# First values ahead of the bias rows on GpSimd's queue, queries first, two weight blocks in halves, and a new order of steps

**Chip and metric.** One core of one Trainium2 chip. The metric is the device time of one execution in microseconds (us). A "look" is one profiled run, of which the start and duration of every instruction are known. "Full rate" and "half rate" name two speeds of the matrix array that are read from durations here: the same fill matmul takes 0.39 us in one stretch and 0.61 us in another.

## The reference, cut to what matters

```python
# attention: B, H, S, D = 8, 8, 576, 64
scores = q @ k.T / 8 + bias_table[bucket(|i - j|)]       # T5 relative bias, per head
attn   = softmax(scores);  x = (attn @ v) as [4608, 512]
# feed-forward, d_ff = 1536
out = ((x @ w_a) * (x @ w_b)) @ w_out
```

The kernel works on bf16. It takes exp of the scores without the bias on ScalarE and multiplies by exp(bias) on VectorE. These factors ("band rows") are loaded from a small table that the kernel itself writes to memory at the start.

## The kernel before

All loads that change fp32 to bf16 are issued from GpSimd's queue, in the order of the tokens that begin with `<`. The other tokens are steps, issued in this order to each engine.

```python
wa_sb = [wpool.tile([128, NMC, WC], BF16, name=f"wa{i}") for i in range(NW)]   # 3 blocks of 512 columns
trb = ps_tr.tile([128, 1024], BF16, tag="tr", name="trb")   # one PSUM tile, used by halves for transposes
# ... cut: helpers
opening = """
    <k0 <q0 <k1 <q123h0 <k23 <tk <W0 <v0 <W1 <vtb <vta <tq <W2 <R0 <v1 <Wta <q123h1 <W3 <Wtb <R1
    <wa0 <k4 <wb0 <R2 <R3 <q4 <k5 <uq <q7 <q5 <wa1 <wb1 ...
    TK0 PC0:A TQ0 ... CK0:A CQ00:D w1 S001 ... E001 E000 ... M001 ... V0:D M101 ... AV00 N00 ...
    ... FA0a N01 HA0a ... FB0a ... FO00 FO01 FO02 HO0 CX70:D CX71:D
"""
```

The tokens that matter: `q0`, `k0`, `v0` are loads of batch 0 (number = head pair or half). `W0..W3` and `R0..R3` are band rows of a pair. `tq`, `tk`, `vta`, `vtb` are tails (the last 64 of 576 positions). `wa0`, `wb0` are weight blocks. `TQ`/`TK`/`TZ`/`X` transpose on TensorE into PSUM (fast memory that TensorE writes to), for the most part into `trb`. `CQ`/`CK`/`CZ`/`CX` copy the result out on ScalarE (`:A`) or VectorE (`:D`). `S` is scores, `E` exponentials (ScalarE), `M` band multiplications (VectorE), `V` a copy of values, `P` pads (writing zeros), `AV` attention times values, `N` its normalisation. `FA`/`FB` are feed-forward products with w_a and w_b, `FO` with w_out, and `wN` is N fill matmuls on zeros.

The softmax here doesn't subtract the row's maximum and nothing guards it: scores larger than these inputs give would overflow.

Of the kernel before, what the change touches and what calls it, by code (L numbers as in the profile page):

```python
# [13 lines left out]
def kernel(  # L14
# [11 lines left out]
    nc = tc.nc  # L26
    FP32 = mybir.dt.float32
    BF16 = mybir.dt.bfloat16
# [13 lines left out]
    NMC = DM // 128  # L42
# [4 lines left out]
    wpool = ctx.enter_context(tc.tile_pool(name="wpool", bufs=1))  # L47
# [17 lines left out]
    half = NB // 2  # L65
# [40 lines left out]

    NW = 3
    WC = DF // NW
    wa_sb = [wpool.tile([128, NMC, WC], BF16, name=f"wa{i}") for i in range(NW)]
    wb_sb = [wpool.tile([128, NMC, WC], BF16, name=f"wb{i}") for i in range(NW)]  # L110
    wo_sb = wpool.tile([128, NDF, DM], BF16, name="wo")
    tab_sb = wo_sb[:, :, :].rearrange("p a b -> p (a b)")[:, 0:TB]
    xn_sb = [wpool.tile([128, NT], BF16, name=f"xn{mc}") for mc in range(NMC)]
# [32 lines left out]
    def load_qh(h0, h1, h):  # L146
        nc.gpsimd.dma_start(
            out=qn[0][64 * h:64 * h + 64, 256 * h0:256 * h1].rearrange("p (h x) -> p h x", x=256),
            in_=q[0, h0:h1, 256 * h:256 * h + 256, :].rearrange("h (p t) d -> p h (t d)", t=NM))
# [4 lines left out]
    def load_v(b, h0, h1):  # L154
        load4(v, vn[b % 2], b, h0, h1)

    def load_compact(b, i):
        nc.gpsimd.dma_start(out=tlc[b][:, i, :].rearrange("r (h d) -> r h d", d=Dh),
                            in_=(q, k)[i][b, :, SM:S, :].transpose([1, 0, 2]))
# [23 lines left out]
    def load_w_out():  # L183
        nc.gpsimd.dma_start(out=wo_sb[:, :, :], in_=moe_w_out.rearrange("(t p) n -> p t n", p=128))
# [32 lines left out]
    def pad_x(i, eng):  # L217
# [5 lines left out]
                        in_=bass.AP(tensor=bias_table.tensor, offset=(NB - 1) * H,  # L223
                                    ap=[[0, NB], [1, H]]))
# [21 lines left out]
    c0 = S - 1 - NR // 2  # L246
# [4 lines left out]
    def load_w(hp, y0, y1):  # L251
        nc.gpsimd.dma_start(out=W_sb[hp][:, :, y0:y1],
                          in_=bass.AP(tensor=tab, offset=2 * hp * TB + y0,
                                      ap=[[NM, 128], [TB, 2], [1, y1 - y0]]))
# [4 lines left out]
    def load_wt(hh):  # L259
        nc.gpsimd.dma_start(out=Wt_sb[64 * hh:64 * hh + 64, :, 64:256],  # L260
                            in_=bass.AP(tensor=tab, offset=hh * TB + 512,
                                        ap=[[1, 64], [2 * TB, H // 2], [1, 192]]))

    def load_vt_part(b, hh):
        nc.gpsimd.dma_start(
            out=vt[b % 2][64 * hh:64 * hh + 64, hh, :, 0:Dh],
            in_=v[b, hh:H:2, SM:S, :].transpose([1, 0, 2]))

    def load_weights(src, dst, part):
        nc.gpsimd.dma_start(  # L270
            out=dst[part][:, :, :],
            in_=src[:, WC * part:WC * part + WC].rearrange("(m p) n -> p m n", p=128))

    def load(name):
        if name[0] in "qk" and name[1:2].isdigit():
            ps, _, half = name[1:].partition("h")
            p0, n = int(ps[0]), len(ps)
            if half:
                load_qh(2 * p0, 2 * p0 + 2 * n, int(half))
            else:  # L280
                b, h = divmod(2 * p0, H)
                (load_q if name[0] == "q" else load_k)(b, h, h + 2 * n)
        elif name[0] in "tu":
            load_compact(int(name[0] == "u"), int(name[1] == "k"))
        elif name in ("v0", "v1"):
            load_v(0, 4 * int(name[1]), 4 * int(name[1]) + 4)
        elif name[:3] == "vb1":
            load_v(1, *((0, 4) if name[3] == "a" else (4, 8)))
        elif name[:2] == "vt":
            load_vt_part(int(name[2] == "1"), "ab".index(name[-1]))  # L290
        elif name == "wo":
            load_w_out()
        elif name[:2] == "Wt":
            load_wt("ab".index(name[2]))
        elif name[0] in "WR":
            load_w(int(name[1]), *((320, NY) if name[0] == "W" else (0, 320)))
        else:
            load_weights(*((moe_w_a, wa_sb) if name[1] == "a" else (moe_w_b, wb_sb)), int(name[2]))

    st = [dict() for _ in range(NP)]  # L300

# [248 lines left out]
    def av(p, jqs):  # L550
        av_mm(p, jqs)
        av_norm(p, jqs)
# [71 lines left out]
    def ff_bank(name):  # L624
        ff["n"] += 1
        if ff["late"] and ff["n"] % 4 >= 2:
            return ps_sc.tile([128, 2, 512], FP32, tag="sc", name=name)[:, 0, :]
        return ps_ff.tile([128, 512], FP32, tag="ffn", name=name)

    def ff_in(w, kind, c, df, lo, n):  # L630
        ps = ff_bank(f"{kind}{c}_{df}_{lo}")
        for mc in range(NMC):
            nc.tensor.matmul(out=ps[:, 0:n], lhsT=w[df // 4][:, mc, 128 * (df % 4):128 * (df % 4) + 128],  # L633
                             rhs=xn_sb[mc][:, 512 * c + lo:512 * c + lo + n],
                             start=(mc == 0), stop=(mc == NMC - 1))
        ff[kind, df, lo] = ps
# [8 lines left out]
    def ff_a(c, df, lo=0, n=512):  # L645
        ff_in(wa_sb, "pa", c, df, lo, n)
        ff_ha(c, df, lo, n)

    def ff_b(c, df, lo=0, n=512):
        ff_in(wb_sb, "pb", c, df, lo, n)  # L650
        ff_g(c, df, lo, n)
# [66 lines left out]
    def v_next(s):  # L718
# [7 lines left out]
    ACT = nc.scalar  # L726

    opening = """
        <k0 <q0 <k1 <q123h0 <k23 <tk <W0 <v0 <W1 <vtb <vta <tq <W2 <R0 <v1 <Wta <q123h1 <W3 <Wtb <R1
        <wa0 <k4 <wb0 <R2 <R3 <q4 <k5 <uq <q7 <q5 <wa1 <wb1 <k6 <uk <vt1b <k7 <vb1a <vb1b <vt1a <wa2 <q6  # L730
        <wb2 <wo TK0 PC0:A TQ0 PF1:D PX1:D PV1:A PU0:D CK0:A CQ00:D w1 S001 PX0:D CQ01:A S000 E001 E000
        w1 TQ30 PC1:D TK1 CK1:D TQ10 CQ10:D S011 E011 CQ30:D TK3 S100 E100 TZ1 CK3:D S301 M001 TQ20
        PV0:D TK2 E301 S101 E101 CQ20:D CK2:D w1 S200 E200 CZ1:D M000 w1 KS w1 S201 EK w2 S010 E201 V0:D
        M101 TZ0 M100 M200 M201 AV00 N00 CZ0:A AV10 E010 X00 CX00:A S300 E300 N10 T0 V1:D X10 CX10:A
        M010 ET0 AV20 TQ11 TQ21 M011 N20 CQ11:A S110 S111 CQ21:A E110 X20 M301 TQ31 M300 AV30 T1 PW:D
        MT0 AV01 CX20:D M110 E111 N30 ET1 X30 M111 CQ31:A T2 ET2 S210 CX30:D E210 PF0:A LH FA0a N01 HA0a
        MT1 TK4 X01 T3 AV11 ET3 CX01:D S211 PU1:D FB0a FA1a E211 CK4:D HA1a N11 X11 G0a M210 S310 MT2
        CX11:A E310 FB1a G1a S311 FA2a HA2a TQ4 M211 CQ4:A FB2a AV21 E311 FA3a HA3a TQ5 MT3 M310 S43 S42
        CQ5:A G2a FB3a N21 M311 TK5 E43 E42 TZ0x G3a CZ0x:D AV31 LV CK5:D N31 FA4a HA4a X21 TQ7 CQ7:A
        S41 E41 S52 E52 CX21:D FB4a FA5a HA5a X31 G4a TK6 M43 FB5a CX31:D S40 E40 S53 G5a FA0b FB0b  # L740
        CK6:D M41 TZ1x HA0b G0b CZ1x:D S51 FA1b FB1b E53 M53 HA1b G1b E51 TK7 CK7:D M40 FA2b HA2b S50
        E50 FB2b FA3b G2b HA3b V2:D T4 FB3b FA4b V3:D ET4 G3b S70 E70 M42 MT4 M52 HA4b FB4b G4b TQ6 T5
        ET5 M50 CQ6:A AV40 N40 MT5 M51 FA5b S71 E71 HA5b S73 FB5b AV41 G5b M70 N41 S72 E73 FA6f E72 T6
        M73 M71 HA6f FB6f G6f AV50 N50 S62 ET6 MT6 E62 S61 FA7f HA7f M62 AV51 N51 TH S60 E61 M61 FB7f
        G7f E60 M60 S63 E63 M63 FA8f HA8f M72 T7 FB8f G8f AV60 N60 ET7 MT7 FA9f HA9f FB9f G9f AV70 FA10f
        FB10f N70 HA10f G10f AV71 FA11f N71 FB11f X71 HA11f G11f AV61 N61 X70 FO00 FO01 FO02 HO0 CX70:D
        CX71:D
    """

    h0 = (0, 1)  # L750
# [2 lines left out]
    def step(token):  # L753
# [5 lines left out]
        if token[0] == "<":  # L759
            load(token[1:])  # L760
            return
# [4 lines left out]
        if kind in ("FA", "HA", "FB", "G"):  # L766
            unit = (0, int(num[:-1]), 256 if num[-1] == "b" else 0, 512 if num[-1] == "f" else 256)
            if kind in ("FA", "FB"):
                ff_in(*((wa_sb, "pa") if kind == "FA" else (wb_sb, "pb")), *unit)
                nxt += 1  # L770
            else:
                (ff_ha if kind == "HA" else ff_g)(*unit)
            return
# [82 lines left out]
    for s in range(8, NP + 1):  # L856
        new = s < NP
        U = "unit"
        A = lambda *jq: (lambda: av(s - 1, jq) if s > 8 else None)
# [20 lines left out]
        b = s // 4 + 1  # L880
# [13 lines left out]
        for x in steps:  # L894
            if x is U:
                seen += 1
                n = (quota * seen + nu - 1) // nu - put
# [35 lines left out]
```

## Time and profile before

| | before |
|---|---|
| time, median of 4 runs | 413.96 us (413.32 to 414.21) |
| span of the profiled run | 412.2 us |
| TensorE busy | 404.5 us, one wait after 30 us (0.17 us, at 224.36) |
| first band multiplication | 11.69 us |
| first attention-value product / first feed-forward matmul | 17.32 / 26.55 us |
| first product with w_out (end of the opening list) | 70.65 us |

After the opening list both programs are the same. A win in the opening should therefore move the end by that much, unless it is given back inside the list. The profile lines behind the table stand in the prediction, but for that of the end of the list (TensorE), which stands behind it, and that of the multiplication (VectorE):

```profile
11.69 0.69 DVE L461 TENSOR_TENSOR ath<-ath,W 128x1024 bf16<-128x1024 bf16 x1
```

```profile
70.65 2.75 PE L670 MATMUL po<-wo,g 128*128 128x512 bf16 x12
...
224.36 1.02 PE L633 MATMUL pb<-xn,wb 128*128 128x512 bf16 x4 [0.17 <-DVE g L643]
```

### The profile page before, as it was taken

The numbers are of one execution on the slowest core, as the hardware profiler recorded it, in microseconds if no ns is written. First come the engines' busy times: TensorE is split into PE (matmuls) and PEld (weight loads), VectorE is DVE, ScalarE is ACT, GpSimd is POOL, SyncE is SP. The second block draws the span as 40 slices with busy tenths as digits, with TensorE's granted clock in tenths as the row PEclk, the third lists the DMA queues.
The fourth block names the chain that finished last, engine by engine and source line by source line (L and its number), as shares of the span: only waits on it lengthen the run. The fifth ranks groups of instructions, "written<-read, shape, count | busy, mean of one in ns | idle before, by whom it ended". The sixth has DMA issues, their size and how long they took to land.

```text
span 412.2 us, 8768 instructions
## 1 busy us (share of the span) xinstructions
PE 404.5 (98%) x3473; PEld 210.0 (51%) x3473; DVE 240.8 (58%) x568; ACT 251.3 (61%) x384; POOL 133.6 (32%) x191
## 2 busy tenths in 40 slices
PE   8999999999999999999999999999999999999996
PEld 3576656455555455455444555555545554444443
DVE  3898997366745665476656764667547652421320
ACT  4998992676748665677556765767486642322321
POOL 6967547788029300960079004300000000000000
PEclk9999999999999999999999999999999999999999
DMA  8999999999979914995299709960520012002004
GB/s 104 179 202 189 206 166 144 160 193 142 87 133 159 139 34 91 155 129 90 41 161 143 116 16 126 127 92 17 117 67 16 17 40 78 0 9 95 2 2 102
DMA packets 135786, 42.05 MB, mean 102 GB/s; under 512 B 113688, under 2 KB 130968, under 8 KB 135744
## 3 DMA queue, kind: packets, MB, share of 16 engines
q0 software_dynamic: 81712, 20.27, 56.3%
q1 hardware_dynamic: 48592, 11.87, 18.6%
q10 hardware_dynamic: 5440, 9.34, 7.2%
q8 instruction: 27, 0.44, 0.5%
q14 instruction: 15, 0.12, 0.1%
HBM read 39.18 MB, written 9.45 MB: 118 GB/s over the span
## 4 chain that ended last, share of the span: by engine, by line
PE 94%; DVE 2%; ACT 2%; DMA 1%; issue 1%; ACTq 0%; POOL 0%; POOLq 0%
PE pb L633 23%; PE pa L633 23%; PE po L670 22%; PE av L569 8%; PE qk L406 7%; PE av L559 2%; PE av L563 2%; PE qkh L446 1%; PE qkt L479 1%; DMA qn<-in_q_dram 1%; PE trb L321 1%; ACT ath L452 1%; PE trb L415 1%; PE trb L609 0%; DVE ath L461 0%
## 5 line engine op out<-in xcount | busy, mean ns | idle before, releaser
L430 ACT ACTIVATE at<-qk 128x1024 bf16<-128x1024 f32 x112 | 113.3, 1028 | 27.5 <-DMA out_dram<-ob 10.3
L643 DVE TENSOR_TENSOR g<-pb,ha 128x512 bf16<-128x512 f32 (+1 forms) x114 | 75.6, 664 | 75.0 <-PE pb L633 58.9
L633 PE MATMUL pb<-xn,wb 128*128 128x512 bf16 (+1 forms) x456 | 112.1, 368 | 0.2 <-DVE g L643 0.2
L633 PE MATMUL pa<-xn,wa 128*128 128x512 bf16 (+1 forms) x456 | 112.1, 368 | 0.0
L640 ACT ACTIVATE ha<-pa 128x512 f32<-128x512 f32 (+1 forms) x114 | 66.2, 581 | 67.7 <-PE pa L633 66.2
L670 PE MATMUL po<-wo,g 128*128 128x512 bf16 x420 | 98.2, 379 | 0.0
L435 DVE TENSOR_TENSOR at<-at,W 128x1024 bf16<-128x1024 bf16 x112 | 75.1, 686 | 22.2 <-ACT at L430 22.1
L633 PEld LDWEIGHTS <-wa 128*128 128x128 bf16 x456 | 41.2, 98 | 46.3 <-issue 6.6
L633 PEld LDWEIGHTS <-wb 128*128 128x128 bf16 x456 | 40.6, 97 | 43.6 <-issue 5.2
L670 PEld LDWEIGHTS <-g 128*128 128x128 bf16 x420 | 38.9, 98 | 44.9 <-issue 2.5
L675 ACT ACTIVATE ob<-po 128x512 f32<-128x512 f32 x34 | 20.4, 600 | 39.9 <-PE po L670 33.6
L569 PE MATMUL av<-vm,at 128*128 128x65 bf16 x896 | 41.2, 193 | 0.0
L569 PEld LDWEIGHTS <-at 128*128 128x128 bf16 x896 | 37.4, 97 | 6.3
L132 POOL DMA_DIRECT2D qn<-in_q_dram x48 | 36.4, 807 | 12.0 <-PE qk L406 6.9
L170 POOL DMA_DIRECT2D vt<-in_v_dram x12 | 7.4, 620 | 98.9 <-PE av L563 98.1
L580 DVE RECIPROCAL rc<-av 128x6 f32<-128x6 f32 (+1 forms) x64 | 11.9, 186 | 45.2 <-PE av L569 40.8
L141 POOL DMA_DIRECT2D kn<-in_k_dram x48 | 36.2, 794 | 1.4 <-issue 0.7
L559 PE MATMUL av<-vt,att 128*128 128x130 bf16 x152 | 33.6, 221 | 0.0
L406 PE MATMUL qk<-QB,KB 64*128 64x512 bf16 x192 | 29.1, 381 | 0.0
L582 DVE TENSOR_TENSOR XG<-av,rc 128x384 bf16<-128x384 f32 (+2 forms) x64 | 27.2, 425 | 2.2
L506 ACT ACTIVATE att<-qkt 128x640 bf16<-128x640 f32 x24 | 16.8, 701 | 13.0 <-PE qkt L480 13.0
L559 PEld LDWEIGHTS <-att 128*128 128x128 bf16 x152 | 15.0, 98 | 6.5
(104 smaller groups left out, 327.0 us busy)
## 6 DMA issues: line engine op xcount, KB each, us to landing
out_dram<-ob ACTq DMA_DIRECT2D x31, 256.0 KB, 3.1
vn<-in_v_dram POOLq DMA_DIRECT2D x16, 256.0 KB, 5.8
kn<-in_k_dram POOLq DMA_DIRECT2D x48, 64.0 KB, 5.0
qn<-in_q_dram POOLq DMA_DIRECT2D x48, 64.0 KB, 4.4
wa<-in_moe_w_a_dram POOLq DMA_DIRECT2D x3, 512.0 KB, 7.4
wb<-in_moe_w_b_dram POOLq DMA_DIRECT2D x3, 512.0 KB, 9.2
wo<-in_moe_w_out_dram POOLq DMA_DIRECT2D x1, 1536.0 KB, 15.6
xn<-XG SPq DMA_TRANSPOSE x52, 3.0
```

The source lines that it names most:

```text
L132: nc.gpsimd.dma_start(out=by_tile(qn[b % 2])[:, h0 // 4, t, :, :], in_=q[b, h0:h1, 128 * t:128 * t + 128, :].transpose([1, 0, 2]))
L141: nc.gpsimd.dma_start(out=by_tile(kn[b % 2])[:, h0 // 4, t, :, :], in_=k[b, h0:h1, t:SM:NM, :].transpose([1, 0, 2]))
L406: nc.tensor.matmul(out=ps[:, hh, :], lhsT=kT[r, t, :], rhs=qT[r, :, :], start=True, stop=True)
L430: nc.scalar.activation(out=at[:, :, :], in_=ps[:, :, :], func=ACTF.Exp, scale=scale)
L435: nc.vector.tensor_tensor(out=at[:, :, :], in0=at[:, :, :], in1=w[:, :, S - 1 + t:S - 1 + t - SM:-1], op=MULT)
L559: nc.tensor.matmul(out=pav[:, slot, :, :], lhsT=weights_tail(p, jq), rhs=vt[i][:, :, hp, :], start=True, stop=True)
L569: nc.tensor.matmul(out=pav[:, slot, hh, :], lhsT=weights(p, t, hh, jq), rhs=vm[i][:, 2 * hp + hh, t, :], start=False, stop=True, skip_grou ...
L582: nc.vector.tensor_tensor(out=xg[:, jqs[0]:jqs[0] + m, :, :], in0=pav[:, 0:m, :, 0:Dh], in1=rc[:, 0:m, :].unsqueeze(3).to_broadcast([128, ...
L633: nc.tensor.matmul(out=ps[:, 0:n], lhsT=w[df // 4][:, mc, 128 * (df % 4):128 * (df % 4) + 128], rhs=xn_sb[mc][:, 512 * c + lo:512 * c + lo ...
L640: nc.scalar.activation(out=ha[:, 0:n], in_=ff["pa", df, lo][:, 0:n], func=ACTF.Copy)
L643: nc.vector.tensor_tensor(out=g_sb[df][:, lo:lo + n], in0=ff["pb", df, lo][:, 0:n], in1=ff["ha", df, lo][:, 0:n], op=MULT)
L670: nc.tensor.matmul(out=po[:, :], lhsT=g_sb[df][:, 128 * tt:128 * tt + 128], rhs=wo_sb[:, df, :], start=(df == 0), stop=(df == NDF - 1))
```

## The change

The intent: with the values there early, the copy of values and all multiplications follow one another without a wait. The bias table's write (GpSimd waits 2.66 us for it) is covered by more loads. The first half of the first w_a block and of the first w_b block comes in time for an earlier feed-forward start.

```diff
-    wa_sb = [wpool.tile([128, NMC, WC], BF16, ...) for i in range(NW)]
+    wa_sb = [wpool.tile([128, 1 + (i == 0), NMC, WC // (1 + (i == 0))], BF16, ...) for i in range(NW)]
     (wb_sb alike; load_weights and ff_in index the halves)
     opening = """
-    <k0 <q0 <k1 <q123h0 <k23 <tk <W0 <v0 <W1 <vtb <vta <tq <W2 <R0 <v1 <Wta <q123h1 <W3 <Wtb <R1
-    <wa0 <k4 <wb0 <R2 <R3 <q4 <k5 <uq <q7 <q5 <wa1 <wb1 ...
+    <q0 <k0 <q123h0 <tk <k1 <k23 <tq <v0 <W0 <W1 <W2 <vta <W3 <q123h1 <vtb <R0 <v1 <Wta <Wtb <wa0a
+    <k4 <R1 <wb0a <R2 <k5 <q4 <wa0b <q5 <uq <wb0b <R3 <q7 <wa1 <vt1b <wb1 ...
-    TK0 PC0:A TQ0 ... CK0:A CQ00:D w1 S001 PX0:D CQ01:A S000 E001 E000 ...
+    PC0:D PF1:A PV0:D w1 TQ0 PU0:A PU1:D TK0 CQ00:A CQ01:A PX1:A CK0:D w1 S001 PV1:D E001 TQ10 ...
+    ... V0:D S200 E200 w2 S201 E201 M000 M001 w2 S300 ... (cut: the same steps in another order,
+    9 fill matmuls instead of 7, 13 copies and pads on the other engine)
+    ... TK5 S42 E311 G2a S43 M310 N21 CK5:D FB3a CZ0x:A FA4a ...
```

More of the change, by code (lines that the diff above doesn't have):

```diff
@@ L108 @@
     WC = DF // NW
-    wa_sb = [wpool.tile([128, NMC, WC], BF16, name=f"wa{i}") for i in range(NW)]
-    wb_sb = [wpool.tile([128, NMC, WC], BF16, name=f"wb{i}") for i in range(NW)]
+    wa_sb = [wpool.tile([128, 1 + (i == 0), NMC, WC // (1 + (i == 0))], BF16, name=f"wa{i}")
+             for i in range(NW)]
+    wb_sb = [wpool.tile([128, 1 + (i == 0), NMC, WC // (1 + (i == 0))], BF16, name=f"wb{i}")
+             for i in range(NW)]
     wo_sb = wpool.tile([128, NDF, DM], BF16, name="wo")
@@ L267, in load_vt_part, with load_weights @@
             in_=v[b, hh:H:2, SM:S, :].transpose([1, 0, 2]))
-    def load_weights(src, dst, part):
+    def load_weights(src, dst, part, half):
+        c0 = WC * part + WC // 2 * half
+        n = WC // (1 + (part == 0))
         nc.gpsimd.dma_start(
-            out=dst[part][:, :, :],
-            in_=src[:, WC * part:WC * part + WC].rearrange("(m p) n -> p m n", p=128))
+            out=dst[part][:, half, :, :],
+            in_=src[:, c0:c0 + n].rearrange("(m p) n -> p m n", p=128))
     def load(name):
@@ L297, in load @@
         else:
-            load_weights(*((moe_w_a, wa_sb) if name[1] == "a" else (moe_w_b, wb_sb)), int(name[2]))
+            load_weights(*((moe_w_a, wa_sb) if name[1] == "a" else (moe_w_b, wb_sb)), int(name[2]), int(name[-1] == "b"))
     st = [dict() for _ in range(NP)]
@@ L628, in ff_bank, with block @@
         return ps_ff.tile([128, 512], FP32, tag="ffn", name=name)
+    def block(w, df, mc):
+        half, d = divmod(df % 4, 2) if df < 4 else (0, df % 4)
+        return w[df // 4][:, half, mc, 128 * d:128 * d + 128]
     def ff_in(w, kind, c, df, lo, n):
@@ L632, in ff_in @@
         for mc in range(NMC):
-            nc.tensor.matmul(out=ps[:, 0:n], lhsT=w[df // 4][:, mc, 128 * (df % 4):128 * (df % 4) + 128],
+            nc.tensor.matmul(out=ps[:, 0:n], lhsT=block(w, df, mc),
                              rhs=xn_sb[mc][:, 512 * c + lo:512 * c + lo + n],
@@ L728 @@
     opening = """
-        <k0 <q0 <k1 <q123h0 <k23 <tk <W0 <v0 <W1 <vtb <vta <tq <W2 <R0 <v1 <Wta <q123h1 <W3 <Wtb <R1
-        <wa0 <k4 <wb0 <R2 <R3 <q4 <k5 <uq <q7 <q5 <wa1 <wb1 <k6 <uk <vt1b <k7 <vb1a <vb1b <vt1a <wa2 <q6
-        <wb2 <wo TK0 PC0:A TQ0 PF1:D PX1:D PV1:A PU0:D CK0:A CQ00:D w1 S001 PX0:D CQ01:A S000 E001 E000
-        w1 TQ30 PC1:D TK1 CK1:D TQ10 CQ10:D S011 E011 CQ30:D TK3 S100 E100 TZ1 CK3:D S301 M001 TQ20
-        PV0:D TK2 E301 S101 E101 CQ20:D CK2:D w1 S200 E200 CZ1:D M000 w1 KS w1 S201 EK w2 S010 E201 V0:D
@@ L734 @@
-        M101 TZ0 M100 M200 M201 AV00 N00 CZ0:A AV10 E010 X00 CX00:A S300 E300 N10 T0 V1:D X10 CX10:A
-        M010 ET0 AV20 TQ11 TQ21 M011 N20 CQ11:A S110 S111 CQ21:A E110 X20 M301 TQ31 M300 AV30 T1 PW:D
-        MT0 AV01 CX20:D M110 E111 N30 ET1 X30 M111 CQ31:A T2 ET2 S210 CX30:D E210 PF0:A LH FA0a N01 HA0a
-        MT1 TK4 X01 T3 AV11 ET3 CX01:D S211 PU1:D FB0a FA1a E211 CK4:D HA1a N11 X11 G0a M210 S310 MT2
-        CX11:A E310 FB1a G1a S311 FA2a HA2a TQ4 M211 CQ4:A FB2a AV21 E311 FA3a HA3a TQ5 MT3 M310 S43 S42
@@ L739 @@
-        CQ5:A G2a FB3a N21 M311 TK5 E43 E42 TZ0x G3a CZ0x:D AV31 LV CK5:D N31 FA4a HA4a X21 TQ7 CQ7:A
-        S41 E41 S52 E52 CX21:D FB4a FA5a HA5a X31 G4a TK6 M43 FB5a CX31:D S40 E40 S53 G5a FA0b FB0b
-        CK6:D M41 TZ1x HA0b G0b CZ1x:D S51 FA1b FB1b E53 M53 HA1b G1b E51 TK7 CK7:D M40 FA2b HA2b S50
-        E50 FB2b FA3b G2b HA3b V2:D T4 FB3b FA4b V3:D ET4 G3b S70 E70 M42 MT4 M52 HA4b FB4b G4b TQ6 T5
-        ET5 M50 CQ6:A AV40 N40 MT5 M51 FA5b S71 E71 HA5b S73 FB5b AV41 G5b M70 N41 S72 E73 FA6f E72 T6
@@ L744 @@
-        M73 M71 HA6f FB6f G6f AV50 N50 S62 ET6 MT6 E62 S61 FA7f HA7f M62 AV51 N51 TH S60 E61 M61 FB7f
-        G7f E60 M60 S63 E63 M63 FA8f HA8f M72 T7 FB8f G8f AV60 N60 ET7 MT7 FA9f HA9f FB9f G9f AV70 FA10f
-        FB10f N70 HA10f G10f AV71 FA11f N71 FB11f X71 HA11f G11f AV61 N61 X70 FO00 FO01 FO02 HO0 CX70:D
-        CX71:D
+        <q0 <k0 <q123h0 <tk <k1 <k23 <tq <v0 <W0 <W1 <W2 <vta <W3 <q123h1 <vtb <R0 <v1 <Wta <Wtb <wa0a
+        <k4 <R1 <wb0a <R2 <k5 <q4 <wa0b <q5 <uq <wb0b <R3 <q7 <wa1 <vt1b <wb1 <q6 <k6 <uk <vb1b <vb1a
@@ new lines @@
+        <k7 <vt1a <wb2 <wa2 <wo PC0:D PF1:A PV0:D w1 TQ0 PU0:A PU1:D TK0 CQ00:A CQ01:A PX1:A CK0:D w1
+        S001 PV1:D E001 TQ10 TQ30 S000 E000 S011 E011 PX0:D TK1 CQ10:D CQ30:D TQ20 TZ1 CK1:D CQ20:D S101
+        E101 CZ1:D S100 PF0:D TK2 CK2:D E100 TK3 KS CK3:D EK w1 S301 E301 TZ0 V0:D S200 E200 w2 S201
+        E201 M000 M001 w2 S300 E300 w2 S010 AV00 CZ0:A E010 M100 M101 AV10 M200 TQ21 TQ11 CQ11:A CQ21:A
+        T0 ET0 S110 E110 M301 M201 M300 N00 X00 N10 X10 CX10:A V1:D M011 AV20 M010 CX00:A PW:D AV30 N20
@@ new lines @@
+        S111 E111 MT0 T1 ET1 X20 N30 TQ31 LH AV01 CX20:D X30 T2 S210 M111 CX30:A FA0a FB0a CQ31:A M110
+        ET2 TK4 N01 HA0a MT1 X01 E210 S211 FA1a E211 G0a CX01:D AV11 HA1a CK4:D TQ4 CQ4:A T3 ET3 FB1a
+        FA2a M210 TQ5 HA2a N11 X11 G1a CQ5:A S310 M211 S311 E310 FB2a CX11:D FA3a HA3a TZ0x MT2 AV21 MT3
+        TK5 S42 E311 G2a S43 M310 N21 CK5:D FB3a CZ0x:A FA4a E43 X21 E42 TQ7 M311 AV31 LV G3a HA4a PC1:A
+        CX21:D S41 E41 S52 CQ7:D FB4a FA5a E52 N31 X31 G4a HA5a S40 E40 M41 CX31:D FB5a G5a S53 V3:D
@@ new lines @@
+        FA0b M40 FB0b HA0b TZ1x G0b E53 TK6 CK6:D FA1b FB1b HA1b S51 E51 CZ1x:D S50 FA2b HA2b G1b M43
+        FB2b T4 FA3b E50 HA3b TK7 M42 G2b M53 CK7:D FB3b FA4b G3b ET4 V2:D MT4 S70 E70 M50 M51 FB4b HA4b
+        G4b TQ6 T5 ET5 AV40 N40 FA5b CQ6:A M52 S71 E71 MT5 HA5b S73 FB5b AV41 N41 S72 G5b E73 M71 E72
+        M73 M72 FA6f T6 AV50 ET6 FB6f S62 N50 HA6f G6f E62 S61 MT6 M62 FA7f HA7f AV51 N51 TH S60 E61 M61
+        FB7f E60 S63 E63 G7f FA8f HA8f T7 ET7 M60 FB8f M63 AV60 M70 G8f MT7 N60 FA9f FB9f HA9f G9f AV70
@@ L748 @@
+        N70 FA10f FB10f HA10f G10f AV71 FA11f FB11f N71 X71 HA11f G11f AV61 X70 FO00 FO01 FO02 N61
+        CX70:D HO0 CX71:D
     """
```

## The prediction

> **What bounds the kernel now.** I first read the page's shares and 40 slices: TensorE is busy 404.5 of 412.2 us and only its first slice is below 9 tenths. Then I split the start into stretches of 10 us, columns: matmul, weight load, VectorE, ScalarE, GpSimd (busy us and count), clock, DMA share, GB/s.
>
> ```profile
> PE 404.5 (98%) x3473; PEld 210.0 (51%) x3473; DVE 240.8 (58%) x568; ACT 251.3 (61%) x384; POOL 133.6 (32%) x191
> ...
> 0.00:10.00 10.00, 7.95 (x58) 3.23 (x58) 3.74 (x19) 5.14 (x8) 6.29 (x13) 1.00 0.84 103
> 10.00:20.00 10.00, 9.29 (x123) 5.27 (x120) 8.74 (x21) 8.84 (x12) 10.00 (x15) 1.00 1.17 183
> 20.00:30.00 10.00, 9.27 (x172) 7.22 (x170) 9.48 (x29) 9.03 (x14) 6.27 (x10) 1.00 1.25 196
> 30.00:40.00 10.00, 10.00 (x142) 6.97 (x140) 8.90 (x29) 8.87 (x16) 7.45 (x11) 1.00 1.38 189
> ```
>
> From 30 us on TensorE has no gap, so what counts is how early it gets there. "Busy" flatters the start, because it includes fill matmuls on zeros and matmuls at a low rate. The timeline of TensorE (start, duration in us) shows both:
>
> ```profile
> 6.20 0.64 PE L321 MATMUL trb<-ident,qn 128*64 128x128 bf16 x8 [0.86 <-DMA qn<-in_q_dram]
> ...
> 8.33 0.61 PE L237 MATMUL warm<-zero_sb 128*128 128x512 bf16 x1
> ...
> 13.88 0.39 PE L237 MATMUL warm<-zero_sb 128*128 128x512 bf16 x1
> ...
> 17.32 0.23 PE L559 MATMUL av<-vt,atk 128*128 128x130 bf16 x1
> ...
> 22.31 0.61 PE L446 MATMUL qkh<-QT,KT 64*128 64x256 bf16 x8 [0.64 <-ACT QT L311]
> ...
> 26.55 0.61 PE L633 MATMUL pa<-xn,wa 128*128 128x256 bf16 x4
> ```
>
> Two of these are landmarks: the first attention-value product (17.32) and the first feed-forward matmul (26.55). At full rate, by start-to-start distances later in the same timeline, the real work ahead of 17.32 is: 4 key transposes x 0.35, 1 whole query transpose 0.35, 3 half query transposes x 0.25, 9 score halves x 0.33, two tail transposes 0.44, tail keys 0.44, together 6.4 us. So about 11 us of the first 17.3 are lost. From 17.32 to 26.55 four gaps (18.6, 20.3, 21.7 and scraps) lose about 1.6 us more. From 26.55 to the end of the opening list (73.4) I count 45.6 us of work in 46.85 us, so at most 1.2 us are lost there. All that a new opening can win lies in these some 13 us, and most of it is the unavoidable arrival of data.
>
> What fills the time to 26 us is ScalarE, which takes every exponential:
>
> ```profile
> 8.01 1.94 ACT L452 ACTIVATE ath<-qkh 128x1024 bf16<-128x1024 f32 x2 [0.28 <-PE qkh L446]
> 10.79 3.05 ACT L452 ACTIVATE ath<-qkh 128x1024 bf16<-128x1024 f32 x3 [0.84 <-PE qkh L446]
> 13.99 1.94 ACT L452 ACTIVATE ath<-qkh 128x1024 bf16<-128x1024 f32 x2 [0.16 <-PE qkh L446]
> ```
>
> From 8.0 it is nearly unbroken at 0.96 us per exponential. VectorE is nearly unbroken from 9.9 us at 0.65 us per band multiplication. The chain of waits agrees: 4.09 us of the query load, then scores, exponentials, one multiplication, a normalisation. On GpSimd's queue:
>
> ```profile
> 8.31 0.72 POOL L252 DMA_DIRECT2D W<-bias_tab  x1 [2.66 <-DMA bias_tab<-wo]
> 9.02 0.78 POOL L123 DMA_DIRECT2D vn<-in_v_dram  x1
> ```
>
> GpSimd stands 2.66 us until the bias table is in memory, then issues one load per 0.72 us.
>
> **What the Trainium skill says.** "DMA: Bandwidth & Descriptors", section "SWDGE vs HWDGE vs iDMA": a DMA that casts can only be issued from GpSimd. All these loads turn fp32 into bf16 or stand in one queue with such, so order on that queue is the lever; the trace agrees that they are all GpSimd's. Same page, "Issuing engines are not separate DMA queues": all issues end on the same 16 engines. The trace shows the sharing, at a DMA share of 1.17 in 10 to 20 us: a load issued earlier takes its place ahead of another, it doesn't come free. "TensorE: Matmul & The Clock Gate", Part 1: the array starts at half rate and needs a busy window of about 3.4 us. The fill matmul's 0.61 us at 8.33 and 0.39 at 13.88 agree in kind, but full rate comes only at some 13.9 us here, 12.7 us after the first matmul, and the row of granted clock shows nothing of it.
>
> **The change, part by part.**
> Loads. No bytes added; two more issues (the first two weight blocks in halves). Before the table wait there are now 8 loads instead of 6 (tail queries and the first values move ahead). The wait ends at 8.31 in both kernels, since its origin (table, cast at 3.85, store) is untouched. So later issues come 2 x 0.72 = 1.4 us earlier: band rows of pair 2 from 12.4 to 9.75, those of pair 3 from 15.9 to 11.1, late queries from 15.2 to 11.9, first weight half from 17.9 to 16.1. But the first band rows now queue behind 64 + 256 KB more. In the trace the first six loads (896 KB) had landed by about 10.6 us, each 128 KB taking some 0.85 us; 320 KB more make 2.1 us. So band rows of pair 0, which landed 3.1 us after issue (11.4), should land near 13.5. The first multiplication (11.69) goes to about 14.1. That is the price of the change.
>
> Start. Queries now come first, keys second; scores need both, the second load still lands at about 6.2, and the first exponential stays at 8.0.
>
> ScalarE. Ahead of the first feed-forward matmul it has the same 15 large exponentials (15 x 0.96 = 14.4 us). Walking the new list with the old durations I get small gaps of 0.2, 0.3 and 0.35 us in place of 0.84 + 0.16 + 0.2 + 0.3: second tail of exponentials ends near 25.3 (before 25.6), then the copy for the last pair's rows, at 25.65, and the third tail ends near 26.9 (before 27.3). Some pads and one copy leave it, some come.
>
> VectorE. Before the first normalisation it now does 8 multiplications instead of 6, from 14.1: values 0.5 ahead, then 8 x 0.65 = 5.2, so the first normalisation is near 19.3 (before 18.53). But two multiplications more are then done (1.3 us), which leaves a lead of about 0.5 us. From there: second normalisation, second values, two multiplications, third normalisation 23.2, tail multiplication 23.9.
>
> TensorE. The sets of real work ahead of the first feed-forward matmul are the same in both lists (I compared them token by token). Two fill matmuls more cost 0.4 us of time in which it waits anyway. The second half of the first pair's values product waits for the tail multiplication, 23.9, lasts 0.95, then 0.12 + 0.40 + 0.33 of transposes and scores: first feed-forward matmul at about 25.7 instead of 26.55, a lead of 0.85. After it the list puts feed-forward pieces earlier, which want first weight halves: I put their landings near 22.5 (A) and 25.5 (B), so the second can cost up to 0.3 us. The second half of B comes after five loads more than the whole block did before: 608 KB at the 156 KB/us of 21.3 to 28.7 us are 3.9 us, so it lands between 31 and 32.5, and it is wanted near 32.
>
> Sum: about 0.85 won at the first feed-forward matmul, perhaps 0.4 of the later 1.2 us of scraps, less about 0.25 for weights or queries that come late: 1.0 us. After the opening list the programs are the same. 414.04 - 1.0 = 413.0 us.
>
> **The rivals.** One: the band rows decide. If they land at 14.5 or later, VectorE, already 8.7 of 10 us busy between 10 and 20, can't catch up; normalisations slip by 1 us and the time is 414 to 415. For it: the DMA share above 1. Against it: 8 multiplications then run back to back, where the old ones had 2.15 us of idleness before 9.9 and a wait of 0.46 for an exponential. Two: late weights and queries of batch 1. The old trace shows GpSimd itself held up behind weight landings (1.77 us before 25.61, 1.95 us before 28.97), so DMA is the limit from 18 to 40 us; every wait that TensorE takes there counts in full, 414 to 416. Against it: bytes are the same and start up to 1.4 us sooner. Three: everything fits; ScalarE has no gap from 8.0 on. 8.0 + 14.4 + 1.8 of copies = 24.2, a lead of 2.3 us, and with the scraps 411. I give the three some 0.2, 0.15 and 0.2; the rest is the middle.
>
> **Range and chances.** The floor is rival three, 411; the ceiling rivals one and two, up to 415. Repeats spread by 0.9 us. Eight in ten: 411.3 to 414.7. For 2%, 8.3 us would have to be won out of 13 lost, while ScalarE alone holds 24.2; or some load would have to be 8 us late in a queue of unchanged bytes. I give 1.5% to faster and 1.5% to slower.
>
> **What would show it.** Right: first band load still issued at 8.3 behind an idle time of about 1.2 us; first multiplication near 14; first exponential at 8.0; first feed-forward matmul between 25.2 and 26.2; the three feed-forward output groups that close the list about 1 us sooner than 70.8 us; the rest shifted alike. Wrong: a first feed-forward matmul past 26.5, waits of TensorE on weights, queries or band rows between 25 and 40 us, or a shift that the later part gives back or adds to.

## More of the kernel before

Only runs of the fast state are compared. All runs here were of that state.

## The result

| | before | after |
|---|---|---|
| time, median of 4 runs | 413.96 (413.32 to 414.21) | 413.14 (412.56 to 414.04) |
| span of the profiled run | 412.2 | 410.8 |
| first exponential | 8.01 | 6.86 |
| first band multiplication | 11.69 | 13.12 |
| first feed-forward matmul | 26.55 | 24.07 |
| first product with w_out | 70.65 | 69.55 |

The ratio is 0.9984, with 95% interval 0.9963 to 1.0006. A ratio here is the mean time of one kernel's fast runs over that of the other's in the same rounds, so it is not quite the ratio of the medians. Two later repeats of the kernel after gave 0.9976 (0.9956 to 0.9995) and 0.9969 (0.9942 to 0.9995). The gain is small, about 1 us, and in the first measurement it is not clear of the noise.

The timeline of TensorE in the kernel after (start and duration in us, with idle time before and its releaser in brackets) answers the lines of the prediction:

```profile
5.80 0.39 PE L239 MATMUL warm<-zero_sb 128*128 128x512 bf16 x1
...
16.55 0.22 PE L563 MATMUL av<-vt,atk 128*128 128x130 bf16 x1 [0.26 <-DMA vt<-in_v_dram]
...
24.07 0.61 PE L641 MATMUL pa<-xn,wa 128*128 128x256 bf16 x4
24.52 0.60 PE L641 MATMUL pb<-xn,wb 128*128 128x256 bf16 x4
...
35.17 0.33 PE L613 MATMUL trb<-ident,XG 128*128 128x128 bf16 x3 [0.67 <-ACT ZB L315]
...
69.55 2.75 PE L678 MATMUL po<-wo,g 128*128 128x512 bf16 x12
```

The feed-forward start is 2.48 us sooner, with exactly the same real work ahead of it, but the end of the list is only 1.10 us sooner. More than half of the lead is lost between 24 and 70 us. The line at 35.17 is the one long wait of TensorE in there. After the list 0.33 us come back: the kernel before waits at 224.36 us for VectorE's product `g`, and the kernel after does not. This holds in every look. From the first product with w_out to the end the five looks at the old list take 341.5 to 341.6 us, the nine at the new one 341.2 to 341.3. Why the list decides this so much later isn't shown. ScalarE's, VectorE's and GpSimd's timelines of the same run:

```profile
6.86 4.74 ACT L456 ACTIVATE ath<-qkh 128x1024 bf16<-128x1024 f32 x5 [0.17 <-PE qkh L450]
```

```profile
12.59 0.62 DVE L317 COPY vm<-vn 128x1024 bf16<-128x1024 bf16 x1 [0.52 <-DMA vn<-in_v_dram]
13.12 4.92 DVE L465 TENSOR_TENSOR ath<-ath,W 128x1024 bf16<-128x1024 bf16 x8
```

```profile
8.16 2.12 POOL L254 DMA_DIRECT2D W<-bias_tab  x3 [1.03 <-DMA bias_tab<-wo]
```

The first five exponentials follow without a gap, and eight multiplications do so behind the copy of values. GpSimd waits 1.03 us for the table instead of 2.66.

### The profile page after: what moved, and what is told of

Its sections match the earlier page's. It is cut to its first block, busy times and chain, and to the rows that moved or that the text cites. A ratio compares the mean times of both kernels' runs of the same rounds, so it can differ in the third digit from the quotient of the medians.

```text
span 410.8 us, 8719 instructions
## 1 busy us (share of the span) xinstructions
PE 399.3 (97%) x3424; PEld 208.9 (51%) x3475; DVE 240.6 (59%) x567; ACT 251.5 (61%) x385; POOL 135.1 (33%) x193
## 4 chain that ended last, share of the span: by engine, by line
PE 92%; DMA 2%; issue 1%; DVE 1%; POOL 1%; ACT 1%; ACTq 0%; POOLq 0%
PE pb L641 23%; PE pa L641 23%; PE po L678 22%; PE av L573 8%; PE qk L410 7%; PE av L563 2%; PE av L567 2%; DMA vn<-in_v_dram 1%; PE qkt L483 1%; DMA bias_tab<-wo 1%; POOL W L254 1%; PE trb L419 1%; PE trb L325 1%; PE warm L239 1%; PE qkt L489 0%
## 5 line engine op out<-in xcount | busy, mean ns | idle before, releaser
L641 PE MATMUL pa<-xn,wa 128*128 128x512 bf16 (+1 forms) x440 | 110.8, 368 | 0.7
L678 PE MATMUL po<-wo,g 128*128 128x512 bf16 x403 | 95.5, 379 | 0.8
```

What stands on the lines that cost most here:

```text
L641: nc.tensor.matmul(out=ps[:, 0:n], lhsT=block(w, df, mc), rhs=xn_sb[mc][:, 512 * c + lo:512 * c + lo + n], start=(mc == 0), stop=(mc == NM ...
L678: nc.tensor.matmul(out=po[:, :], lhsT=g_sb[df][:, 128 * tt:128 * tt + 128], rhs=wo_sb[:, df, :], start=(df == 0), stop=(df == NDF - 1))
```

## The experiments

Twelve runs were made, of nine other kernels and three repeats, all with correct results. One comparison carries most of them: the span minus the start of the first feed-forward matmul, that is, how long everything after that landmark takes.

| run | first feed-forward | span | difference | ratio to before (95%) |
|---|---|---|---|---|
| before / before_again | 26.55 / 26.48 | 412.2 / 412.6 | 385.6 / 386.1 | - / 0.9993 (0.9974, 1.0013) |
| before_fill | 25.89 | 411.9 | 386.0 | 0.9993 (0.9972, 1.0014) |
| halves_on_before | 26.92 | 412.6 | 385.7 | 0.9990 (0.9965, 1.0015) |
| loads_only | 27.21 | 412.9 | 385.7 | 1.0006 (0.9980, 1.0032) |
| after / after_again / after_third | 24.07 / 24.26 / 25.49 | 410.8 / 410.9 / 412.2 | 386.7 / 386.6 / 386.7 | 0.9984 / 0.9976 / 0.9969 |
| after_nofill | 24.50 | 411.2 | 386.7 | 0.9987 (0.9968, 1.0005) |
| keys_first | 24.84 | 411.5 | 386.7 | 0.9992 (0.9967, 1.0018) |
| bands_first | 26.96 | 413.7 | 386.7 | 1.0017 (0.9989, 1.0044) |
| list_only | 29.42 | 416.1 | 386.7 | 1.0082 (1.0058, 1.0105) |
| whole_blocks | 24.45 | 414.8 | 390.3 | 1.0060 (1.0036, 1.0084) |
| cz_early | 25.49 | 410.9 | 385.4 | 0.9954 (0.9930, 0.9978) |

The difference is nearly constant for a list of steps. It is 385.6 to 386.1 for the old one, whose upper values are the looks in which TensorE waited 0.3 to 0.4 us for the second weight block. It is 386.7 for the new one where the weights come in halves. So the new list, with its own loads, reaches its landmark sooner and then takes 0.6 to 1.1 us longer. Within the list (landmark to first product with w_out) it takes 0.9 to 1.4 us longer, 45.5 against 44.1 to 44.6, and the 0.33 us above come back later. The landmark itself moves by over 1 us from look to look of one program.

### Noise first: both kernels again

No edit.

> The kernel before, unchanged: a null test and a second look at when TensorE comes to full rate. If the moment is fixed by the program's own gaps, the fill matmul near 8.3 us again takes 0.6 us and the one near 13.9 us 0.4 us, and the first feed-forward matmul is again at 26.5 us (within 0.3). If the moment drifts from run to run, it comes at another time, and the landmark moves by up to 1 us. Ratio to the kernel before 1.000 within 0.003.

Measured: 413.58 us, ratio 0.9993. Full rate came at another time. The fill matmul at 5.93 us took 0.61 us, the one at 7.43 us took 0.39, and later ones (13.12, 14.21) took 0.61 again. The array had gone to full rate at some 6.5 us and fallen back near 11. In the first look it was at half rate until 13.9 us. Yet the landmark is the same, 26.48 against 26.55. In this kernel the moment of full rate did not set the start of the feed-forward part.

> The kernel after, unchanged. If its early full rate (a fill matmul of 0.39 us at 5.8 us) belongs to the program, it is there again, first exponential at 6.9 us, first feed-forward matmul at 24.1 us (within 0.3), ratio 0.997. If it was luck of the run, full rate comes later by some microseconds, the first exponential is near 7.5 to 8 us and the ratio is nearer 0.999 to 1.000.

Measured: 412.66 us, ratio 0.9976, with the early full rate again, first exponential at 6.77 and landmark at 24.26. A third look came:

> The kernel after again, beside the next three on the same chip: first feed-forward matmul at 24.1 to 24.3, first output group at 69.5 to 69.8, wait of 0.67 us of TensorE at 35.2 for ScalarE's copy of the tails, ratio 0.9975 within 0.001.

Measured: 412.99 us, ratio 0.9969, but in its profiled run (413.96 us) the landmark is at 25.49 and the first product with w_out at 70.96. Both miss the expectation. Here is the same stretch of TensorE's timeline in after_again and in after_third:

```profile
5.37 0.41 PE L325 MATMUL trk<-ident,kn 128*64 128x128 bf16 x8 [0.24 <-DMA kn<-in_k_dram]
...
10.70 0.64 PE L325 MATMUL trk<-ident,kn 128*64 128x128 bf16 x16
```

```profile
6.39 0.41 PE L325 MATMUL trk<-ident,kn 128*64 128x128 bf16 x8 [0.84 <-DMA kn<-in_k_dram]
...
11.72 1.07 PE L325 MATMUL trk<-ident,kn 128*64 128x128 bf16 x16
```

The keys, issued at 2.07 us in both, landed 3.3 us later in one and 4.3 in the other. In the late run the array also went back to half rate (16 transposes in 1.07 us instead of 0.64). In this look the landmark came 1.2 to 1.4 us later. The late keys and the half rate are the two things that differ. Both arose in an unchanged program, and no run sets one without the other, so their shares aren't shown. Times of this program in other executions weren't profiled.

### Does the fill matmul carry the gain?

```diff
- TK0 PC0:A TQ0            (kernel before)
+ TK0 PC0:A w2 TQ0
```

> The kernel before with two fill matmuls more, between the first key and the first query transposes, where TensorE stood idle for 0.86 us. Theory (the gap kept the array at half rate until 13.9 us): full rate comes near 5 to 8 us, transposes and scores before 13.9 us take two thirds of their time, first feed-forward matmul at 25.3 to 26.0 instead of 26.55, ratio 0.997 to 0.999. Rival (loads and the order of work set the start, the rate does not matter): first feed-forward matmul within 0.2 us of 26.55, ratio 1.000.

Measured: full rate from 5 to 11.4 us, landmark 25.89, as the theory had it, but the ratio is 0.9993 with an interval that holds 1, and before_again had full rate over nearly the same stretch without a sooner landmark. One look doesn't settle 0.6 us against a spread of over 1 us.

```diff
- PV0:D w1 TQ0 PU0:A       (kernel after)
+ PV0:D TQ0 PU0:A
```

> The kernel after without the one fill matmul that stands ahead of the first query transposes. Theory: TensorE gets a gap of about 0.4 us before 5.2 us and perhaps misses its busy window: half rate until 8 us or later, first exponential at 7.3 to 8 us, first feed-forward matmul 0.4 to 1 us later than 24.07. Rival (loads and order set the start): full rate or not, first feed-forward matmul within 0.2 us of 24.07.

Measured: half rate until 5.9 us and again from 9.2 us, first exponential 6.94, landmark 24.50, inside what the three looks at the kernel after show. Its time is 413.35 us, ratio 0.9987 against 0.9976. The theory that the fill carries the gain has no support. At most some tenths are its share.

### Which part does it: loads, list, halves, values

```diff
  (loads of after, steps of before)
```

> The new order of loads with the halved weight blocks, the old list of steps (it still transposes keys first). Theory (the gain is of the new step list, whose fill matmul and query-first order keep TensorE busy from 1.2 us): keys, now loaded second, leave a gap ahead of the first transposes, half rate until late, first exponential near 8, and the first feed-forward matmul at 26.0 to 26.8, ratio 0.999 to 1.002. Rival (the order of loads is the gain): first feed-forward matmul near 25, ratio 0.996 to 0.998.

Measured: landmark 27.21, a little later than expected, ratio 1.0006. The theory also missed at the start: the array was at full rate from 5.75 us, and the first exponential came at 7.33, not near 8. The new order of loads alone wins nothing. The old list's first multiplication now waits 1.42 us for its band rows, as the price in my prediction had it, and three key transposes wait 2.7 us in all for keys.

```diff
  (loads of before, whole blocks; steps of after)
```

> The old order of loads with whole weight blocks, the new list of steps. Theory: queries, now loaded second, come after the keys, TensorE gets a gap ahead of its first transposes, and late band rows and weights (first weight block issued near 17.9, second near 19.4) hold up the new list, which asks for both sooner: first feed-forward matmul near 25.5 to 27, its partner up to 29, ratio 1.000 to 1.005. Rival (the list alone is the gain): first feed-forward matmul near 24.5, ratio 0.997.

Measured: landmark 29.42, worse than my worst case, time 417.66 us. The new list on the old loads waits where it wants band rows of pair 3 early. VectorE's timeline of list_only:

```profile
20.32 1.30 DVE L461 TENSOR_TENSOR ath<-ath,W 128x1024 bf16<-128x1024 bf16 x2 [2.37 <-DMA W<-bias_tab]
```

In the kernel after all eight multiplications have run by 18 us. Neither part is a gain by itself. The list is written for its loads.

```diff
- <wa0a ... <wb0a ... <wa0b ... <wb0b      (kernel after)
+ <wa0  ... <wb0
```

> The kernel after with its first two weight blocks whole again, each issued where its first half was. Theory (the halves matter because the transfers are the limit from 16 us on): the second block, twice as long, lands 1.5 to 2.5 us later than its half did and the second feed-forward matmul waits 0.5 to 2 us; end 0.3 to 1 us later than the kernel after. Rival (the halves are hidden): landmarks within 0.2 us, ratio as the kernel after, 0.997 to 0.998.

Measured: 416.62 us, ratio 1.0060. The wait came as expected, but the cost was some 3.5 us. TensorE's timeline of whole_blocks shows a second term:

```profile
27.08 0.61 PE L633 MATMUL pb<-xn,wb 128*128 128x256 bf16 x4 [2.02 <-DMA wb<-in_moe_w_b_dram]
...
28.57 1.02 PE L633 MATMUL pa<-xn,wa 128*128 128x256 bf16 x4
...
31.16 0.64 PE L321 MATMUL trb<-ident,qn 128*64 128x128 bf16 x8
```

The wait of 2.02 us was followed by about 3.5 us at half rate (four matmuls in 1.02 us where others take 0.61, eight transposes in 0.64 where others take 0.41). The second w_b product starts at 32.26 instead of 28.40 in after_again: 3.86 us. Of these, 0.19 are the later landmark, about 2.2 the wait (start to start) and about 1.5 the stretch at half rate. "TensorE: Matmul & The Clock Gate", Part 1 of the Trainium skill, states that the array falls back to half rate after an idle window of about 3.4 us. Here the fall came 1.5 us after a wait of only 2.02 us. That the wait caused it isn't shown: in after_third the array fell back at 8.86 us with no wait of TensorE above 0.84 us before it, and in before_again near 11 with none above 0.96.

```diff
- <wa0 <k4 <wb0 <R2 <R3 <q4 <k5 <uq                      (kernel before)
+ <wa0a <k4 <wb0a <R2 <R3 <q4 <k5 <wa0b <wb0b <uq
```

> The kernel before with its first two weight blocks in column halves, the first halves where the whole blocks stood, the second ones three and four loads later; steps unchanged. Theory (the halves pay only for a list that asks for weights at 24 us; the old one asks for the second block at 29.4, when the whole block has just landed): first feed-forward matmul within 0.3 us of 26.5, the wait of 0.3 to 0.4 us for the second block, seen in one look at the kernel before, is gone, ratio 0.999 to 1.001. Rival (halves are the gain by themselves): ratio 0.997.

Measured: 413.87 us, ratio 0.9990, landmark 26.92 (0.4 later, a miss by 0.1), no wait for weights. On the old list the halves are worth nothing that can be measured. The new one can't do without them.

```diff
- <v0 <W0 <W1 <W2 <vta     (kernel after)
+ <W0 <W1 <W2 <v0 <vta
```

> The kernel after with the first values behind the band rows of pairs 0 to 2. My prediction held that values ahead delay the first band rows by 2 us. If so, the first band rows land earlier than they did, the first multiplication comes before 13.1 and is preceded by the copy of values, which now waits till about 14; as the list has that copy ahead, the multiplications start 1 to 2 us later than 13.12, first feed-forward matmul up to 1 us later, ratio 0.998 to 1.001. Rival (ScalarE sets the pace, VectorE has slack): first feed-forward matmul within 0.3 us of 24.07, ratio 0.997.

Measured: 414.47 us, ratio 1.0017, landmark 26.96. The direction is as expected and the size is not: the multiplications began at 15.97, 2.85 us later than 13.12 where I allowed 1 to 2. The landmark is 2.9 us past the earliest look at the kernel after and 1.5 past its latest, which had equally late keys; I allowed 1 us. VectorE's timeline of bands_first:

```profile
15.63 0.43 DVE L317 COPY vm<-vn 128x1024 bf16<-128x1024 bf16 x1 [2.69 <-DMA vn<-in_v_dram]
```

The first band rows landed 3.2 us after issue here and 4.9 in the kernel after, so values ahead do delay them by 1.7 us. But what stands at the head of the new list is the copy of values, and it waits 2.69 us with the bands first. As the list is written, it needs the values ahead. A list with the copy of values further back wasn't tried.

```diff
- <q0 <k0 <q123h0          (kernel after)
+ <k0 <q0 <q123h0
```

> The kernel after with its first two loads swapped, keys first, steps as they are. Theory (query first matters little, as scores need both and the second lands at the same time): first query transposes wait till near 5.4 as in the run with the old loads, first exponential within 0.3 us of 6.8 to 6.9, first feed-forward matmul within 0.3 us of 24.2. Rival (query first is what brings the first exponential forward): first exponential at 7.3 or later, first feed-forward matmul 0.5 us later or more.

Measured: first exponential 7.77, landmark 24.84, ratio 0.9992 against 0.9969. By the exponential the rival is right, yet after_third, with queries first, had its first exponential at 7.79. The array was also at half rate here. What queries first are worth stays open: the intervals overlap, and one landing moves more than the swap.

### Why the lead is given back

In all looks at the new list ScalarE stands idle before it copies the tail transposes of batch 1. The timeline of ScalarE in after_third:

```profile
33.13 1.02 ACT L456 ACTIVATE ath<-qkh 128x1024 bf16<-128x1024 f32 x1
35.77 0.77 ACT L315 ACTIVATE ZB<-trb 64x256 bf16<-64x256 bf16 x2 [1.63 <-DVE KT L317]
```

It waits for VectorE's copy of the next keys, whose data it doesn't need. Both read the one transpose tile, and the list has VectorE's copy ahead. The old list had the tail copy on VectorE too, ahead of the copy of keys, and TensorE has no wait there.

```diff
- TK5 S42 E311 G2a S43 M310 N21 CK5:D FB3a CZ0x:A FA4a      (kernel after)
+ TK5 S42 E311 CZ0x:A G2a S43 M310 N21 CK5:D FB3a FA4a
```

> The kernel after with one step earlier in the list: ScalarE's copy of batch 1's tail transposes now stands ahead of VectorE's copy of the next keys instead of behind it. Theory (the lead is given back because both copies read the one transpose tile and are held in the order of the list, so ScalarE idles 1.63 us behind VectorE): that idle time falls under 0.3 us, TensorE's 0.67 us at 35.2 and 0.23 us at 38.9 go, the first output group comes 0.5 to 1.0 us sooner than in the kernel after, ratio 0.995 to 0.9965. Rival (ScalarE and VectorE lack time there anyway): the waits move to another copy and the first output group comes within 0.2 us of the kernel after.

Measured: 412.42 us, ratio 0.9954 (0.9930 to 0.9978), the fastest kernel here. The times alone don't separate it from after_third (0.9942 to 0.9995); the traces do. The profiled runs of after_third and cz_early are alike from the landmark (25.49 in both) to 33 us, so this is a clean pair. ScalarE in cz_early:

```profile
33.12 1.02 ACT L456 ACTIVATE ath<-qkh 128x1024 bf16<-128x1024 f32 x1
34.44 0.77 ACT L315 ACTIVATE ZB<-trb 64x256 bf16<-64x256 bf16 x2 [0.30 <-PE trb L325]
```

The idle time falls from 1.63 to 0.30 us. TensorE's waits of 0.67 and 0.23 us are gone. The first product with w_out starts at 69.70 instead of 70.96, and the span is 410.9 instead of 412.2. The miss: the gain at that product is 1.26 us, more than the 1.0 I allowed, and more than the 0.90 of the two waits together. Start to start, cz_early is ahead by 0.80 us at the first wait, gains 0.11 in score matmuls that ran faster (0.61 against 0.72), 0.30 at the second wait and 0.05 in scraps. So the order of the two copies decides. That the shared tile is the reason isn't tested, as no run gave the copies two tiles.

## Why the prediction was right, and where not

The number was right (413.0 against 413.14, and 412.66 and 412.99 in the repeats), but two of its terms were wrong by about 1 us each, in opposite directions. That they made up for each other was luck. (413.0 was worked out from 414.04, the median of the three runs of the kernel before that were known then, not from 413.96.) Of its signs of being right, two came: the first load of band rows, issued at 8.16 behind 1.03 us of waiting, and the list's end about 1 us sooner. The first exponential and the first multiplication came sooner than stated, and the first feed-forward matmul before its range in two of three looks. A sign of being wrong came too: a shift that the later part gives back. "From 30 us on TensorE has no gap" overlooked the wait at 224.36.

- **The first exponential at 8.0** failed. It came at 6.86, 6.77 and 7.79. I took the landing of the second load (6.2 us) from one look. It lands 3.2 to 4.3 us after issue, before_again has an early exponential too (7.17), and the timeline of one look can't tell a program's property from its luck.
- **The price of values ahead** was right in its mechanism (band rows 1.7 us later after issue; I had worked out 2.1) and too large in its effect. The multiplications began at 12.66 to 13.51 us instead of 14.1 and did not wait on band rows in the three looks. That was close: in the first look the rows landed 0.06 us before the multiplication, and in whole_blocks, with the same list and the same loads ahead, it waited 0.41 us for them. The wait that counted was that for the values themselves, as bands_first shows.
- **The first feed-forward matmul at 25.7, lead 0.85** was mis-sized: 24.07, 24.26 and 25.49, a mean of 24.6, against 26.5 for the two looks at before, so a lead of 1.9 us. Of my range for it (25.2 to 26.2) only one look is inside. Rival three had the landmark near 24.2, where two looks are, but from a first exponential at 8.0. What share the early first exponential has isn't shown: in before_again it came 0.84 us sooner than in before, and the landmark stayed.
- **"Perhaps 0.4 of the later 1.2 us of scraps", less 0.25 for late loads** had the wrong sign. Between the landmark and the end of the list the new list loses 0.9 to 1.4 us instead of winning 0.15, and 0.33 us come back at 224 us, so that it takes 0.6 to 1.1 us longer from the landmark on (386.7 against 385.6 to 386.1). The cause was none of my rivals, neither weights nor queries nor band rows, but the order of two copies out of one PSUM tile. cz_early shows it: one token moved makes it 385.4.
- **The loads fit** was right, and only just. The first w_b half, issued at 17.77 and landing 6.3 us later, is there at 24.1, and TensorE asks for it at 24.52. With whole blocks some 3.6 us are lost (390.3 against 386.7).

So 1.9 won before the landmark less about 0.9 given back after it make 1.0, where I had written 0.85 plus 0.15.

What stays open is how the 1.9 us divides among early keys, the array's rate, and the list. The looks are few, and one program's landmark moves by over 1 us between them. Open too is why the old list's wait at 224 us is gone with the new one.

## What to carry to other kernels

A hand-ordered list and its order of loads are one thing. Each alone made this kernel slower or left it as it was, and the pair gained 1 us. When a landmark moves by more than the end does, subtract it from the span: the rest was constant to 0.1 us for the new list here and to 0.5 us for the old, and it led to the one misplaced copy. Where two engines copy out of one shared tile, look in the trace whether one is held behind the other, and try the other order. Here ScalarE stood 1.63 us behind a copy that it didn't need, and moving its own copy ahead brought 1.26 us at the end of the list.

## What the Trainium skill lacked or had wrong

- "TensorE: Matmul & The Clock Gate", Part 1, ties the fall to half rate to an idle window of about 3.4 us. In whole_blocks it came 1.5 us after the end of a wait of 2.02 us and cost some 1.5 us more. In after_third it came at 8.86 us with no wait of TensorE above 0.84 us before it. The same Part, "A second HAM failure mode", describes falls from frequent short idle times; whether these are such falls is open, as no run here tests it.
- Same page, Part 1: the page has a kernel's start at half rate and then warm, run-variable by the phase of the window. Here one program was at half rate until 13.9 us in one look, and in another at full rate from 6.5 to about 11 us and then at half rate again. The landmark was 26.55 and 26.48, so the moment of full rate did not move the landmark there.
- "DMA: Bandwidth & Descriptors", "Anatomy of one DMA", gives a fit of 2.0 us plus bytes over 436 GB/s. For the first loads (128 KB written, 256 KB read) an estimate from it is 2.3 to 2.6 us. The first in an empty queue took 3.1 to 3.3 us from issue to landing, the second 3.2 to 4.3 from run to run.
- No page that I read gives how far the landing of one early load moves from run to run. Here the keys landed 3.3 or 4.3 us after issue in two runs of one program. Their spans were 410.9 and 412.2 us, with the array's rate differing too.
